# Moving 22 weight loads of one stage from SyncE's DMA queue to GpSimd's

## The chip, the cores and the metric

The kernel runs on one core of one Trainium2 chip. The metric is the device time of one execution in microseconds, lower is better. TensorE is called PE here, VectorE DVE, ScalarE ACT, GpSimd POOL and SyncE SP, as in the profile.

## The reference

A block of three parts, all in float32, on 2304 tokens (4 batches of 576) with a model width of 512.

```python
# 1. random-feature attention, 8 heads of 64, 128 features (q, k already scaled)
phi = lambda x: exp(h - max(h)) / sqrt(128)      # h = x @ omega.T - |x|^2 / 2
num = phi(q) @ (phi(k).T @ v);  den = phi(q) @ sum(phi(k)) + 1e-6
x = num / den                                     # 2304 x 512
# 2. a feed-forward net with 2048 hidden columns
h = x @ w_in;  x = (h * sigmoid(h)) @ w_out
# 3. a gated one with 1536 hidden columns
g = x @ w_gate;  x = (g * sigmoid(g) * (x @ w_val)) @ w_out2
```

The weights come as float64, so each number in HBM is two 32-bit words.

## The kernel before

The matrix products of parts 2 and 3 are done with seven half-size products in place of eight (Strassen's scheme in Winograd's form): an operand is cut into four blocks A11, A12, A21, A22, four sums S1 to S4 of them are made, and seven of these pieces are used. Each piece is kept as two TensorE operands, a rounded "hi" and the remainder "lo", and three matmuls (hi·hi, hi·lo, lo·hi) give a float32-like product.

The program runs five stages one after the other: attention (to about 118 us of the span), **up 1** (`x @ w_in`, to about 290 us), down 1 (with `w_out`), up 2 (`w_gate`, `w_val`) and down 2. Up 1 walks over 24 steps (eight column blocks `i` of `w_in` by three token blocks `s`), in the order blocks 0 to 2, then 3, then 4, then 5 to 7, all three token blocks for each group; a step is seven products `p` (order 1, 5, 6, 2, 7, 3, 4) of six matmuls at L1133. Within a step the partial sums in PSUM are copied from bank to bank by ACT (`copy`, L1150) before TensorE may add the next product to them, so an ACT copy that is late stops TensorE.

Beside its products, up 1 converts weights, in the stream "conv" (`conv_job`). One job takes one block of a weight matrix:

- `load(h)`, L344: two DMAs of 512 KB (h = 0 and 1) bring the two-word numbers into a raw buffer. There are two raw buffers, three once the x operands are made (about 162 us).
- `first(h)`, L368 on ACT, then `shift(h)`, L375 and `low(h)`, L382 on DVE: put the two words together to a float32. `low` gives the raw buffer back.
- `sums(n)`, L401 on POOL, four times: S1, S3, S2, S4 into a buffer `S` of which there is one only, so the next job's S1 waits until this job is done with it.
- For a `w_in` block: `hi` (L433 on DVE, L435 on ACT) and `lo` (L448 on DVE) make the operands that up 1 uses soon after. For a `w_out`, `w_gate` or `w_val` block: `store` (L465, three DMAs on SP) puts the pieces to a DRAM scratch, to be loaded again later.

The jobs in up 1 are in 3, out 3, in 4, out 4, in 5, out 5, in 6, out 6, in 7, out 7, gate 0, val 0. The two loads of the first, in 3, are issued ahead of the stage.

The order of every engine's instructions is fixed when the program is built. A small model keeps a clock for each engine (`clk`), one for the DMA engines, and times `T` at which pieces are ready; `Stream.best` emits, among the heads of a stream's queues (one queue for each engine, in the order that `weave` gives), the one that can start first. For a load the model takes `t` from the engine's clock, adds 0.35 us of issue, starts the transfer no sooner than `t + 1.55` and adds a margin of 1 us (2.5 us for gate and val) to the end before ACT's `first` is planned. On the chip each engine then runs its list strictly in order and waits on semaphores. `weave` puts the two loads of job n+1 ahead of the sums and stores of job n:

```python
for n, j in enumerate(jobs):
    new = deque(jobs[n + 1][:8] ...)        # load 0, load 1, first 0, first 1, shift, low, ...
    for _ in range(min(2, len(new))): ops.append(new.popleft())
    for i, o in enumerate(j[8:]):           # sums 1, 3, [stores], 2, 4, [store] or hi, lo
        ops.append(o)
        if i % 2 and new: ops.append(new.popleft())
    ops += new
```

So SP's queue of the stream holds loads and stores, POOL's holds the sums. SP also issues, in the same list, all other transfers: the results of up 1 (`put`, L1159, `g_d`), the weights of down 1 from the scratch (`down_ops`, L1312, `wd_out`, then L1316 on ACT and L1320 on DVE), and the first inputs of down 1 (`zload`, L1341, only once the stream "conv" is empty; then L1367 on ACT and L1371 on DVE).

Of the kernel before, what the change touches and what calls it, by code (L numbers as in the profile page):

```python
# [11 lines left out]
U32 = mybir.dt.uint32  # L12
# [30 lines left out]
def kernel(  # L43
# [13 lines left out]
    nc = tc.nc  # L57
    ctx.enter_context(tc.manual_schedule())
    P = 128
# [3 lines left out]
    S = 576  # L63
# [16 lines left out]
    FP = (w_in.shape[0], w_gate.shape[0])  # L80
    wsrc = {"in": w_in, "out": w_out, "gate": w_gate, "val": w_val, "out2": w_out2}
    wsrc = {k: w.bitcast(U32) for k, w in wsrc.items()}
# [6 lines left out]
    wd_d = {k: tc.dram_tile([7, P, FP[m] * 256], F32, name=f"wd_{k}") for m, k in enumerate(DNK)}  # L89
    wu_d = {k: tc.dram_tile([P, 7 * 256], F32, name=f"wu_{k}") for k in UPK[1]}  # L90
# [12 lines left out]
    def cut(t, o, n):  # L103
        return t[:, o : o + n]
# [39 lines left out]
    clk = {e: 0.0 for e in ("PE", "ACT", "DVE", "POOL", "SP", "dma", "slot", "landed")}  # L144
# [3 lines left out]
    def cost(kind, n):  # L148
        a, b = fixed[kind]
        return a + b * n  # L150

    class Op:
        __slots__ = ("eng", "cost", "fn", "ins", "outs", "guard", "then", "slots", "live", "lead")

# [20 lines left out]
        def emit(self):  # L175
            t = max(clk[self.eng], self.ready())
            clk["slot"] = 0.0
            if self.eng == "SP":
                took, lag = self.cost
                clk["SP"] = t + 0.35  # L180
                clk["dma"] = max(t + 1.55, clk["dma"]) + took
                clk["end"] = clk["landed"] = clk["dma"] + lag
            else:
                clk["end"] = t + self.cost
            self.fn()
            if self.eng == "SP":
                end = clk["landed"]
            else:
                clk[self.eng] = end = t + self.cost
            for k in self.outs:  # L190
                T[k] = end
            if self.then is not None:
                self.then(end)
# [3 lines left out]
    def dma_cost(nbytes, kind="rows"):  # L197
        a, b = RATE[kind]
        return nbytes * a, b
# [125 lines left out]
    f_raw = Free("raw", [cut(fa, R_AT + i * 1024, 1024) for i in range(2)])  # L325
# [8 lines left out]

    halved = []

    def conv_job(kind, i, dram=None, side=False):
        b = {}
        key = lambda *k: (kind, i, *k)

        def load(h):
            def go():
                b["r", h] = r = f_raw.take()
                nc.sync.dma_start(out=r.bitcast(U32), in_=wsrc[kind][i, h])  # L344

            def then(end):

                if kind != "out2":
                    T[key("r", h)] = end + (1 if kind in ("in", "out") else 2.5)
                else:  # L350
                    T[key("r", h)] = end + 6.0

            return Op("SP", dma_cost(P * 4096, "words"), go, outs=[key("r", h)], slots=(f_raw, 1), then=then)

        def word(h, w):
            return b["r", h].bitcast(U32).rearrange("p (c w) -> p c w", w=2)[:, :, w]
# [32 lines left out]
        def blk(n):  # L389
            if n in ("A21", "A22"):  # L390
                return cut(b["c", 0], 0 if n == "A21" else 256, 256)
            if n in ("A11", "A12"):
                return cut(b["c", 1], 0 if n == "A11" else 256, 256)
            return cut(b["S"], 256 * (int(n[1]) - 1), 256)

        def sums(n, l, r, ins):
            def go():
                if n == 1:
                    b["S"] = f_sum.take()
                f = nc.gpsimd.tensor_add if n == 1 else nc.gpsimd.tensor_sub  # L400
                f(blk(f"S{n}"), blk(l), blk(r))  # L401

            return Op(
                "POOL", cost("POOL", 256), go, ins=[key(*k) for k in ins], outs=[key("S", n)],
                slots=(f_sum, 1) if n == 1 else None,
            )


        parts = ((0, 1), (1, 3), (3, 5), (5, 7))
        after = ([("f", 0)], [("f", 1)], [("S", 1), ("S", 2)], [("S", 3), ("S", 4)])  # L410

        def src(k):
            if k == 0:
                return blk("A22")
            return b["c", 1] if k == 1 else cut(b["S"], 512 * (k - 2), 512)

        def done(t):
            f_c.give(b["c", 0], t)
            f_c.give(b["c", 1], t)
            f_sum.give(b["S"], t)  # L420
# [34 lines left out]
            eng = "POOL" if side else "DVE"  # L455
            return Op(eng, cost(eng, n), go, ins=[key("hi", k)], outs=outs)

        def store(a, z, src, ins):

            b["stores"] = 3  # L460

            def go():
                o = dram(a, z)
                t = src()
                nc.sync.dma_start(out=o, in_=t.rearrange("p (o c) -> p o c", c=256) if len(o.shape) == 3 else t)  # L465
                b["stores"] -= 1
                if not b["stores"]:
                    done(clk["landed"])

            return Op("SP", dma_cost(P * (z - a) * 1024, "parts"), go, ins=[key(*x) for x in ins], outs=[key("d", a)])  # L470

        half = [load(0), load(1), first(0), first(1), shift(0), low(0), shift(1), low(1)]
        if dram is not None:
            return [
                *half,
                sums(1, "A21", "A22", [("f", 0)]),
                sums(3, "A11", "A21", [("f", 0), ("f", 1)]),
                store(0, 1, lambda: blk("A22"), [("f", 0)]),
                store(1, 3, lambda: b["c", 1], [("f", 1)]),
                sums(2, "S1", "A11", [("f", 1)]),  # L480
                sums(4, "A12", "S2", [("f", 1)]),
                store(3, 7, lambda: b["S"], [("S", n) for n in range(1, 5)]),
            ]
        f0, f1 = ("f", 0), ("f", 1)
        return [
# [25 lines left out]
    def weave(*jobs):  # L511

        ops = [*jobs[0][:8]]
        for n, j in enumerate(jobs):
            new = deque(jobs[n + 1][:8] if n + 1 < len(jobs) else ())
            for _ in range(min(2, len(new))):
                ops.append(new.popleft())
            for i, o in enumerate(j[8:]):
                ops.append(o)
                if i % 2 and new:  # L520
                    ops.append(new.popleft())
            ops += new
        return ops

    def down_job(m, i):
        k = DNK[m]
        return conv_job(
            k, i, dram=lambda a, z: wd_d[k][a:z, :, i * 256 : (i + 1) * 256].rearrange("o p c -> p o c")
        )

    def up_job_dram(k):
        return conv_job(k, 0, dram=lambda a, z: wu_d[k][:, a * 256 : z * 256])

    early = {"conv": deque(), "x": deque()}

# [184 lines left out]
    def u_of(u, b):  # L720
        return u // UB, UB * (u % UB) + b
# [185 lines left out]
    def store(u):  # L907
        B, p = u_of(u, 0)
        for b in range(UB):
            T["xd", B, p + b] = 0.0  # L910
            made["xd", B, p + b] = (step_of[0], 3, "out")
        nc.sync.dma_start(
            out=x_d[B][p : p + UB].rearrange("b p s -> p b s"), in_=xts.pop(u).rearrange("p (b s) -> p b s", b=UB)
        )
# [5 lines left out]
    for t in spare_c:  # L920
        f_c.give(t, 0.0)
    f_sum.give(spare_sum, 0.0)
    early["conv"].extend(chain(*(conv_job("in", i, side=True) for i in range(3)), *(down_job(0, i) for i in range(3))))
    early["x"].extend(x_prep(0, 0, xr1, False, "POOL", early=True))
    def two_steps(d):
# [78 lines left out]
    first_up = conv_job("in", 3)  # L1004
    for x in first_up[:2]:
        x.emit()
    for f, some in ((f_c, spare_c), (f_sum, [spare_sum])):
        n = len(f.q)
# [588 lines left out]
        lambda: x_prep(0, 2, xr2, False, "DVE", before=1, then=xr2_end),  # L1597
    ]

    rest = deque(down_job(0, i) for i in range(3, FP[0]))  # L1600
    jobs = []
    for i in range(3, FP[0]):
        jobs += [conv_job("in", i) if i > 3 else first_up, rest.popleft()]
    jobs += rest
    jobs += [up_job_dram("gate"), up_job_dram("val")]
    conv1 = [x for x in weave(*jobs) if not any(x is y for y in first_up[:2])]
    opened = []
    extra_c, extra_raw = cut(fa, XR_AT, 512), cut(fa, XR_AT + 512, 1024)
# [108 lines left out]
    jobs = []  # L1717
    for i in range(1, FP[1]):
        jobs += [conv_job("gate", i), conv_job("val", i), down_job(1, i - 1)]
# [75 lines left out]
```

## Time and profile before

| | |
|---|---|
| three runs | 827.64, 827.8 (median), 830.42 us |
| the profiled execution | 828.38 us, of which the span from first to last instruction is 826.6 us |
| granted TensorE clock | 1.000 of full speed |

The profile shows one execution. "Busy" is the time in which an engine executes; a wait is the idle time of an engine ahead of an instruction, put down to what ended it. Rows marked SPq or ACTq are the engine's sequencer: for a DMA the time that its issue took. Times in a timeline count from the span's start.

### The profile page before, as it was taken

To read this page: it belongs to the slowest core of one execution; us is meant where nothing else is said; L and a number is where in the kernel's file an instruction comes from. 1 tells how busy PE (TensorE), PEld (TensorE's weight loads), DVE (VectorE), ACT (ScalarE), POOL (GpSimd) and SP (SyncE) were. 2 spreads that over 40 slices of the span, in tenths; PEclk is the share of its full clock that TensorE was granted. 3 is DMA by queue.
4 is the path that set the end of the run, shared out by engine and by line. 5 is a ranking of instruction groups with operands and counts; after the bars stand their busy time and mean duration, and the time that the engine had idled before them with its cause. 6 is when DMAs were issued, how large, how long until landed. Compare 5 with 4: busy or idle time off the path is not lost.

```text
span 826.6 us, 18058 instructions
## 1 busy us (share of the span) xinstructions
PE 814.5 (99%) x6889; PEld 794.8 (96%) x6889; DVE 615.1 (74%) x982; ACT 558.5 (68%) x1172; POOL 162.4 (20%) x204
## 2 busy tenths in 40 slices
PE   8999999999999999999999999999999999999998
PEld 7878889999999999999999999999999999999998
DVE  4888877657744598995989987675656559998872
ACT  6989978867767776455577776665656558655552
POOL 0477851033442000000000113130303020000000
PEclk9999999999999999999999999999999999999999
DMA  8679956679889996538366836463636278764502
GB/s 281 197 249 277 315 186 218 201 223 328 288 266 374 395 306 213 170 115 267 116 212 230 271 102 211 126 213 105 212 107 216 101 235 318 250 217 140 164 3 77
DMA packets 112134, 175.58 MB, mean 212 GB/s; under 512 B 9648, under 2 KB 94256, under 8 KB 112048
## 3 DMA queue, kind: packets, MB, share of 16 engines
q1 hardware_dynamic: 111824, 174.20, 63.7%
q8 instruction: 54, 0.88, 0.4%
q10 hardware_dynamic: 224, 0.23, 0.1%
q14 instruction: 32, 0.26, 0.1%
HBM read 109.38 MB, written 65.01 MB: 211 GB/s over the span
## 4 chain that ended last, share of the span: by engine, by line
PE 81%; issue 6%; ACT 4%; DMA 4%; DVE 2%; POOL 1%; SPq 1%; ACTq 0%; DVEq 0%; POOLq 0%
PE ps L1133 36%; PE ps L1556 35%; PE ps L777 3%; ACT kq L793 2%; PE ps L821 2%; PE ps L837 2%; PE ps L868 2%; DMA fa<-in_moe_w_out 1%; POOL fa L401 1%; DMA g_d<-fa 1%; DMA ra<-wd_out 1%; PE ps L893 1%; DMA rawq<-in_q 1%; DVE fa L382 1%; ACT qp L839 1%
## 5 line engine op out<-in xcount | busy, mean ns | idle before, releaser
L401 POOL TENSOR_TENSOR fa<-fa 128x256 f32<-128x256 f32 x124 | 103.4, 848 | 496.2 <-DMA x_d<-fa 202.9
L1133 PE MATMUL ps<-ra 128*128 128x384 f32 x840 | 143.0, 327 | 2.2 <-ACT ps L1150 2.2
L1133 PE MATMUL ps<-rb,ra 128*128 128x384 f32 x840 | 142.4, 327 | 0.8 <-ACT ps L1150 0.8
L1133 PE MATMUL ps<-rc,ra 128*128 128x384 f32 x840 | 141.1, 326 | 0.0
L1133 PEld LDWEIGHTS ps<-ra 128*128 128x128 f32 x840 | 137.1, 189 | 3.5 <-ACT ps L1150 3.5
L1133 PEld LDWEIGHTS ps<-rb,ra 128*128 128x128 f32 x840 | 137.2, 189 | 2.0 <-ACT ps L1150 1.9
L1133 PEld LDWEIGHTS ps<-rc,ra 128*128 128x128 f32 x840 | 137.2, 189 | 0.0
L1150 ACT ACTIVATE ps<-ps 128x384 f32<-128x384 f32 x180 | 85.8, 478 | 67.2 <-PE ps L1133 58.1
L1367 ACT ACTIVATE ra<-fa 128x768 fp32r<-128x768 f32 x81 | 68.0, 843 | 64.2 <-PE ps L1556 55.1
L1556 PE MATMUL ps<-ra,rb 128*128 128x384 f32 x576 | 96.5, 326 | 0.0
L1556 PEld LDWEIGHTS ps<-ra,rb 128*128 128x128 f32 x576 | 94.1, 189 | 0.0
L1371 DVE TENSOR_TENSOR ra<-fa,ra 128x768 fp32r<-128x768 f32 x80 | 76.2, 954 | 19.6 <-ACT ra L1367 18.9
L793 ACT ACTIVATE kq<-ps,nb 128x128 f32<-128x128 f32 x288 | 79.4, 408 | 6.2 <-DVE nb L791 6.1
L1207 DVE TENSOR_TENSOR fa<-fa,ps 128x384 f32<-128x384 f32 x78 | 43.0, 552 | 35.7 <-ACT ps L1150 26.2
L1556 PE MATMUL ps<-ra 128*128 128x384 f32 x414 | 69.2, 326 | 0.0
L1556 PE MATMUL ps<-ra,rc 128*128 128x384 f32 x402 | 68.8, 326 | 0.0
L1556 PEld LDWEIGHTS ps<-ra 128*128 128x128 f32 x414 | 67.6, 189 | 0.0
L1556 PEld LDWEIGHTS ps<-ra,rc 128*128 128x128 f32 x402 | 65.9, 189 | 0.0
L1391 DVE TENSOR_TENSOR fa<-ra,fa 128x768 f32<-128x768 f32 x63 | 60.1, 954 | 0.9 <-DMA ra<-g_d 0.4
L382 DVE SCALAR_TENSOR_TENSOR fa<-fa 128x512 uint32<-128x512 uint32 x65 | 58.7, 903 | 0.7
L368 ACT ACTIVATE fa<-fa 128x512 f32<-128x512 f32 x65 | 54.3, 838 | 4.4 <-DMA fa<-in_moe_w_out 2.7
L791 DVE TENSOR_REDUCE nb<-ps 128x4 f32<-128x512 f32 x72 | 48.4, 682 | 6.3 <-PE ps L777 3.2
(128 smaller groups left out, 1153.2 us busy)
## 6 DMA issues: line engine op xcount, KB each, us to landing
g_d<-fa SPq DMA_DIRECT2D x110, 192.0 KB, 3.8
fa<-g_d SPq DMA_DIRECT2D x42, 384.0 KB, 4.6
ra<-g_d SPq DMA_DIRECT2D x42, 384.0 KB, 4.0
fa<-in_moe_w_out SPq DMA_DIRECT2D x28, 512.0 KB, 5.2
g_d<-mf SPq DMA_DIRECT2D x58, 192.0 KB, 3.9
fa<-in_moe_w_in SPq DMA_DIRECT2D x16, 512.0 KB, 5.2
wd_out<-fa SPq DMA_DIRECT2D x12, 512.0 KB, 3.3
fa<-in_moe_w_gate SPq DMA_DIRECT2D x12, 512.0 KB, 4.1
```

The source lines that it names most:

```text
L368: nc.scalar.activation(c, word(h, 1).bitcast(F32), AF.Prelu, scale=2.0**-112, alpha=-(2.0**32))
L382: nc.vector.scalar_tensor_tensor(c, word(h, 0), 29, c, op0=ALU.logical_shift_right, op1=ALU.bitwise_or)
L401: f(blk(f"S{n}"), blk(l), blk(r))
L791: nc.vector.reduce_max(nb, x, axis=AX.X, negate=True)
L793: nc.scalar.activation(e[:, g // 2, g % 2, h * M : (h + 1) * M], x[:, g, :], AF.Exp, bias=nb[:, g : g + 1])
L1133: nc.tensor.matmul(woven(ps[b][:, :N]), cut(l, j * P, P), halves(cut(r, j * N, N)), start=start and c == 0, stop=stop and c == 5, skip_gro ...
L1150: nc.scalar.activation(out() if callable(out) else out, src, AF.Copy)
L1207: nc.vector.tensor_add(t, t if in_place else p5[n], ps[bank_][:, :N])
L1367: nc.scalar.activation(ops[s, p, k][0], src(), AF.Copy)
L1371: nc.vector.tensor_sub(l, src(), h.bitcast(F32))
L1391: (nc.gpsimd if eng == "POOL" else nc.vector).tensor_sub(z(PLACE[to]), z(PLACE.get(l, l)), z(PLACE.get(r, r)))
L1556: nc.tensor.matmul(woven(ps[BANKS[p] + e][:, :N]), cut(a, e * P, P), halves(b), start=p in FIRST and i == 0 and c == 0, stop=p in LAST and ...
```

## The change

In up 1 the loads of the conversion's words are issued by POOL on its own DMA queue; all other transfers stay on SP's. These are the 22 loads of out 3, in 4 to val 0; those of in 3 are issued ahead of the stage as before, and the conversions in attention and in up 2 keep SP (`own=""`). In the model a load now takes 1.0 us of POOL's clock, and it stands in POOL's queue of the stream, among the sums, in the order that `weave` gives. The code can also put the stores of S (`"S"`) on POOL, which is not used.

```diff
+    ISSUE = {"SP": 0.35, "POOL": 1.0}
...
-            if self.eng == "SP":
+            if isinstance(self.cost, tuple):
                 took, lag = self.cost
-                clk["SP"] = t + 0.35
+                clk[self.eng] = t + ISSUE[self.eng]
                 clk["dma"] = max(t + 1.55, clk["dma"]) + took
...
-    def conv_job(kind, i, dram=None, side=False):
+    def conv_job(kind, i, dram=None, side=False, own=""):
...
                 b["r", h] = r = f_raw.take()
-                nc.sync.dma_start(out=r.bitcast(U32), in_=wsrc[kind][i, h])
+                (nc.gpsimd if "L" in own else nc.sync).dma_start(out=r.bitcast(U32), in_=wsrc[kind][i, h])
...
-            return Op("SP", dma_cost(P * 4096, "words"), go, outs=[key("r", h)], slots=(f_raw, 1), then=then)
+            return Op("POOL" if "L" in own else "SP", dma_cost(P * 4096, "words"), go, outs=[key("r", h)], slots=(f_raw, 1), then=then)
...
-    rest = deque(down_job(0, i) for i in range(3, FP[0]))
+    OWN = "L"
+    rest = deque(down_job(0, i, OWN) for i in range(3, FP[0]))
     jobs = []
     for i in range(3, FP[0]):
-        jobs += [conv_job("in", i) if i > 3 else first_up, rest.popleft()]
+        jobs += [conv_job("in", i, own=OWN) if i > 3 else first_up, rest.popleft()]
     jobs += rest
-    jobs += [up_job_dram("gate"), up_job_dram("val")]
+    jobs += [up_job_dram("gate", OWN), up_job_dram("val", OWN)]
```

## Rows read from the trace of the kernel before

**Rows 1.** The page: span, and busy time of TensorE.

```profile
span 826.6 us, 18058 instructions
...
PE 814.5 (99%) x6889; PEld 794.8 (96%) x6889; DVE 615.1 (74%) x982; ACT 558.5 (68%) x1172; POOL 162.4 (20%) x204
```

**Rows 2.** Waits of PE in up 1, 118 to 292 us (total us, times, longest).

```profile
PE ps L1133 <- ACT ps L1150: 2.5, 5, 1.2
```

**Rows 3.** Timeline of PE in up 1 (start, us, what, idle before).

```profile
190.35 1.24 PE L1133 MATMUL ps<-ra 128*128 128x384 f32 x6 [0.23 <-ACT ps L1150]
...
195.01 1.24 PE L1133 MATMUL ps<-rb,ra 128*128 128x384 f32 x6 [0.50 <-ACT ps L1150]
...
233.52 1.24 PE L1133 MATMUL ps<-ra 128*128 128x384 f32 x6 [1.19 <-ACT ps L1150]
235.04 10.99 PE L1133 MATMUL ps<-ra 128*128 128x384 f32 x66 [0.28 <-ACT ps L1150]
245.87 1.14 PE L1133 MATMUL ps<-rb,ra 128*128 128x384 f32 x6
```

**Rows 4.** Timeline of ACT, same stretch.

```profile
189.06 0.86 ACT L368 ACTIVATE fa<-fa 128x512 f32<-128x512 f32 x1 [0.65 <-DMA fa<-in_moe_w_in]
...
232.42 0.66 ACT L368 ACTIVATE fa<-fa 128x512 f32<-128x512 f32 x1 [2.49 <-DMA fa<-in_moe_w_out]
```

**Rows 5.** Waits of ACT in up 1, 118 to 292 us.

```profile
ACT fa L368 <- DMA fa<-in_moe_w_out: 2.7, 2, 2.5
...
ACT fa L368 <- DMA fa<-in_moe_w_in: 1.3, 2, 0.6
```

**Rows 6.** Timeline of SP's queue, same stretch.

```profile
181.44 0.45 SPq L344 DMA_DIRECT2D fa<-in_moe_w_in  x1
...
218.95 0.33 SPq L344 DMA_DIRECT2D fa<-in_moe_w_in  x1
...
222.00 3.94 SPq L465 DMA_DIRECT2D wd_out<-fa  x2
225.99 0.50 SPq L344 DMA_DIRECT2D fa<-in_moe_w_out  x1
...
228.40 0.44 SPq L344 DMA_DIRECT2D fa<-in_moe_w_gate  x1
```

**Rows 7.** Timeline of POOL, same stretch.

```profile
182.23 2.93 POOL L401 TENSOR_TENSOR fa<-fa 128x256 f32<-128x256 f32 x4 [3.37 <-DMA wd_out<-fa]
...
220.74 4.80 POOL L401 TENSOR_TENSOR fa<-fa 128x256 f32<-128x256 f32 x4 [5.39 <-DVE ra L448]
229.64 2.91 POOL L401 TENSOR_TENSOR fa<-fa 128x256 f32<-128x256 f32 x4 [4.10 <-DMA wd_out<-fa]
```

**Rows 8.** Line L344, 118 to 292 us (ns min/median/max); all its loads to landing.

```profile
L344 SPq DMA_DIRECT2D fa<-in_moe_w_out x10: 333/480/897, 125.0 to 227.8; - x10
...
DMA to landing us min/median/max: 4.2/5.4/7.5
```

**Rows 9.** Line L401, 118 to 292 us (ns min/median/max).

```profile
L401 POOL TENSOR_TENSOR fa<-fa x48: 726/735/2151, 125.0 to 259.2; 128x256 f32<-128x256 f32 x48
```

**Rows 10.** Busy time by stretch: length, PE, PEld, DVE, ACT, POOL; clock, DMA share, GB/s.

```profile
125.00:262.00 137.00, 134.80 (x824) 133.18 (x823) 89.74 (x162) 103.07 (x218) 42.88 (x48) 1.00 0.80 266
```

**Rows 11.** Timeline: last operands of in 7, and the start of down 1.

```profile
235.35 1.03 DVE L448 TENSOR_TENSOR ra<-fa,ra 128x256 fp32r<-128x256 f32 x2 [0.29 <-ACT ra L435]
...
268.26 0.96 DVE L1371 TENSOR_TENSOR mz<-fa,mz 128x768 fp32r<-128x768 f32 x1 [2.14 <-ACT mz L1367]
...
289.81 2.11 PE L1556 MATMUL ps<-mz,ra 128*128 128x384 f32 x12
```

**Rows 12.** Groups of DVE, 118 to 292 us (busy us, mean ns, idle before).

```profile
L382 DVE SCALAR_TENSOR_TENSOR fa<-fa 128x512 uint32<-128x512 uint32 x24 | 22.1, 921 | 0.4
...
L375 DVE TENSOR_SCALAR fa<-fa 128x512 uint32<-128x512 uint32 x24 | 11.9, 497 | 12.2 <-ACT fa L368 11.6 <-DMA g_d<-fa 0.4
...
L433 DVE CAST ra<-fa 128x512 fp32r<-128x512 f32 x10 | 4.2, 424 | 0.1
```

More of the change, by code (lines that the diff above doesn't have):

```diff
@@ L185, in emit @@
             self.fn()
-            if self.eng == "SP":
+            if isinstance(self.cost, tuple):
                 end = clk["landed"]
@@ L456, in lo, with store @@
             return Op(eng, cost(eng, n), go, ins=[key("hi", k)], outs=outs)
-        def store(a, z, src, ins):
+        def store(a, z, src, ins, eng="SP"):
             b["stores"] = 3
@@ L464, in go @@
                 t = src()
-                nc.sync.dma_start(out=o, in_=t.rearrange("p (o c) -> p o c", c=256) if len(o.shape) == 3 else t)
+                by = nc.gpsimd if eng == "POOL" else nc.sync
+                by.dma_start(out=o, in_=t.rearrange("p (o c) -> p o c", c=256) if len(o.shape) == 3 else t)
                 b["stores"] -= 1
@@ L468, in go @@
                     done(clk["landed"])
-            return Op("SP", dma_cost(P * (z - a) * 1024, "parts"), go, ins=[key(*x) for x in ins], outs=[key("d", a)])
+            return Op(eng, dma_cost(P * (z - a) * 1024, "parts"), go, ins=[key(*x) for x in ins], outs=[key("d", a)])
         half = [load(0), load(1), first(0), first(1), shift(0), low(0), shift(1), low(1)]
@@ L481, in conv_job @@
                 sums(4, "A12", "S2", [("f", 1)]),
-                store(3, 7, lambda: b["S"], [("S", n) for n in range(1, 5)]),
+                store(3, 7, lambda: b["S"], [("S", n) for n in range(1, 5)], "POOL" if "S" in own else "SP"),
             ]
@@ L523, in weave, with down_job, up_job_dram @@
         return ops
-    def down_job(m, i):
+    def down_job(m, i, own=""):
         k = DNK[m]
         return conv_job(
-            k, i, dram=lambda a, z: wd_d[k][a:z, :, i * 256 : (i + 1) * 256].rearrange("o p c -> p o c")
+            k, i, dram=lambda a, z: wd_d[k][a:z, :, i * 256 : (i + 1) * 256].rearrange("o p c -> p o c"), own=own
         )
-    def up_job_dram(k):
-        return conv_job(k, 0, dram=lambda a, z: wu_d[k][:, a * 256 : z * 256])
+    def up_job_dram(k, own=""):
+        return conv_job(k, 0, dram=lambda a, z: wu_d[k][:, a * 256 : z * 256], own=own)
     early = {"conv": deque(), "x": deque()}
```

## The prediction, made before the changed kernel was run

> **What bounds the kernel now.** The page comes first: TensorE is busy for 814.5 us of a span of 826.6 us [rows 1]. The change touches up 1 alone, and whatever it does to the queues, it can give back only idle time of TensorE there. So the second view is what TensorE waits for in up 1: 2.5 us in five waits, every one ended by an ACT copy from bank to bank [rows 2]. That is the ceiling of any gain, 0.3% of the time. The third view, TensorE's timeline, places four of them [rows 3]: 0.23, 0.50, 1.19 and 0.28 us, 2.2 us together (the fifth, the rest of 0.3 us, comes after the loads of the stage). The fourth is ACT's timeline ahead of them. At 232.4 us ACT had stood 2.49 us on `first` (L368), because a `w_out` load had not landed; ACT works in order, the copy that TensorE needs came behind it [rows 4], and the gap of 1.19 us follows. The same pattern, smaller, is at 189.1 us: ACT waits 0.65 us on a `w_in` load, TensorE 0.23. In all ACT waits four times on a load, 4.0 us [rows 5], so 18 of 22 land in time. The loads do touch the end, then, but only through ACT's order. A wait of 2.49 us cost 1.19, one of 0.65 cost 0.23 (with work of ACT in between): a copy bears a delay of 0.42 to 1.30 us before TensorE stands. I use the middle, 0.86.
>
> The fifth view says why that load was late. SP's queue stood 3.94 us on two stores of S, until POOL's four sums were done at 220.74 + 4.80 = 225.54, and the load of out 7 came behind them, at 225.99 [rows 6, 7]. It landed at about 232.4, 6.4 us later, where loads of this stretch take 4.2 to 7.5 us, 5.4 in the median [rows 8].
>
> **The change part by part.** It *removes* 22 issues from SP, at 0.33 us (the least) to 0.48 us (a median) each [rows 8], so 7 to 11 us of SP's time. Queued behind them on SP are stores of `g_d` and reloads of the scratch. None of these ends a wait of TensorE in up 1, which are all ACT's copies [rows 2]; as long as that covers them, they are worth nothing.
>
> It *adds* 22 issues to POOL. The trace has no DMA issued by POOL, so the nearest rows bound the price: below, SP's own issue, 0.33 us [rows 8]; above, the longest instruction of POOL in this stage, 2.15 us, where the median is 0.735 [rows 9]. I take 1.0 us: it is the figure in the changed planner, and it lies between a quick and a disturbed POOL instruction. 22 us more are no load for POOL, busy 42.88 of 137 us [rows 10].
>
> It *moves* each load out of SP's list into POOL's, among the sums. There are three kinds; the first loads, of out 3 and in 4, stand ahead of the stretch with the gaps and are left out.
>
> First, the first halves (h = 0) of out 4 to out 7 and val, five loads. They stood behind the store of S, which waits for S4. Now they stand directly behind S4: for out 7 from 225.54 in place of 225.99, 0.45 us sooner, and 0.45 in the other four cases too. The issue takes 1.0 in place of 0.33. So they land later by x = 1.0 - 0.33 - 0.45 = 0.22 us; with the bounds of the issue x runs from -0.45 to 2.15 - 0.33 - 0.45 = 1.37. Where TensorE already waits, x goes through whole. I count three such places, the gaps at 190, 195 and 233 us: 3 × 0.22 = **0.7 us**. Elsewhere 0.22 is under the 0.86 that a copy bears.
>
> Second, the first halves of in 5, in 6, in 7 and gate, four loads. They went out ahead of the sums of the job before and now stand behind them: in 5 went out at 181.44, the sums of in 4 ran from 182.23 to 185.16; gate went out at 228.40, the sums of in 7 ended at 232.55 [rows 6, 7]. That is about 4 us later. What covers it: the second half of the same job goes out later still (in 7's at 218.95, when `low` gives a raw buffer back), and the job's own sums wait for the one buffer S, until 229.64 for in 7. With the issue of 1.0 and the median landing of 5.4 us (counted from SP's issue of 0.33, so 6.1 in all), in 5 lands at 191.3, while ACT's `first` on it ran at 189.06 [rows 4]. In the old order ACT would stand 2.2 us; but the planner knows of the sums and plans `first` later. I take **0**. If that cover is gone, these four pay as in the first rival.
>
> Third, the second halves. Their trigger, `low` of the job ahead, stays, but POOL's next S1 now stands behind the issue. There is room: in 7's second half went out at 218.95, S1 of out 6 began at 220.74, 1.79 us later [rows 6, 7]; in four other cases it is 1.3 to 1.4 us. An issue of 1.0 us fits: **0**. At 2.15 us the chain of sums and stores would be 0.4 to 0.8 us later in each of four rounds, 2.7 us by in 7. In 7's operand for its first product is done by 235.35 + 1.03 = 236.38. That product starts one step, 42 matmuls, ahead of 245.87; 66 took 245.87 - 235.04 = 10.83, so at 245.87 - 6.89 = 238.98 [rows 3, 11]. Its slack of 2.6 us leaves 0.1 us. Down 1 is further off: its first operand is ready at 269.22, used at 289.81 [rows 11].
>
> **The sum.** 0.7 + 0 + 0. The profiled execution took 828.38 us, the span of 826.6 and 1.8 around it; the sum on it gives 829.1. The median of the runs lies 0.6 below that execution, so against the median it is 827.8 + 0.7 = **828.5 us**.
>
> **A rule against this change.** POOL is slower beside DVE: the four sums from 220.74 took 4.80 us, with DVE's conversion running, the four from 229.64 took 2.91 with DVE nearly idle [rows 7]. DVE also has 34 quick instructions in this stage, L375 and L433, at 0.50 and 0.42 us for 512 columns, where L382 takes 0.92 [rows 12]. The Trainium skill (SBUF — State Buffer, "SBUF: two separate sides") says that GpSimd's cores write the descriptors of a DMA issued from there, and that a DVE copy in a two-port mode locks them out until it ends. No row here shows that yet. By that rule alone a load would wait up to one such instruction, 0.43 us, and the time would be 827.8 + 3 × (0.22 + 0.43) = 829.8.
>
> **The rivals.**
>
> *Late loads, ACT stands (slower).* The place is `first` in ACT's list, the price a landing later by x than planned. It meets the nine first halves of the two kinds above: three pay x whole, six pay x - 0.86. At the bound, x = 1.37, that is 3 × 1.37 + 6 × 0.51 = 7.2 us: 835.0. It counts from 3x + 6(x - 0.86) = 4.1 us, which is 0.5%, about what runs of this kernel can tell from no change: x = 1.03, an issue of 1.8 us. For it: no row shows an issue on POOL, and the planner's margin is 1 us. Against: 18 of 22 land in time, and 1.8 us is far from POOL's median of 0.735.
>
> *POOL is slowed beside DVE (a little slower).* The issue stretches as the sums did, by 4.80 / 2.91 = 1.65: x = 1.65 - 0.78 = 0.87, which costs 3 × 0.87 = 2.6 us and 6 × 0.01: 830.5. For it: the two rows of sums. Against: most sums take their least, 0.735 against 0.726 [rows 9].
>
> *Loads overtake stores (a little faster).* On a queue of its own a load no longer stands behind the stores' bytes in SP's. If the one of 6.4 us takes the 4.2 of the quickest [rows 8], it lands 2.2 us sooner, and if the others gain likewise, all four gaps close: 825.6. For it: the spread of the landings. Against: the same engines move the same bytes, and stores that share them end later. The Trainium skill (DMA: Bandwidth & Descriptors, "Issuing engines are not separate DMA queues") holds that only issue time is saved; by it this gain is nothing, and the time 828.5. No row before can show it: these transfers have one queue.
>
> *The move does nothing that counts.* With x near 0 the gaps stay: 827.8, within the forecast.
>
> **How the numbers follow.** Forecast, x between 0 and 0.4: 0.52. Late loads beyond 0.5%: 0.21. POOL slowed: 0.11. Overtaking: 0.14. Something unpriced, to the good side: 0.02. Faster by over 0.5% needs 4.1 us, more than the 2.5 us of idle in up 1: 0.02. Slower by over 0.5% is the first rival: 0.21. The rest, 0.77, is within 0.5%. The range begins at 826.1 (three gaps, 0.23, 1.19 and 0.28, gone) and ends at 833.5, halfway from 831.9, where late loads begin to count, to their upper price.
>
> **What would show it.** POOL's queue should have 22 DMA issues at L344 of about 1.0 us; 0.33, or over 1.8, moves the sum. Out loads should go out as S4 ends, in and gate first halves some 4 us later than before. ACT's waits at L368 on loads should stay under some 6 us, TensorE's in up 1 under 4. S1 of the out jobs should follow the end of L448, not that of an issue. The landing tells overtaking (near 4.2 us) from slowing (over 6). Down 1 should still start near 290 us. The prediction is wrong if TensorE's waits in up 1 pass 6.6 us, or if time is lost elsewhere, as around the span.

## The result and the profile after

The changed kernel takes 832.97 us (median of six runs, 831.71 to 834.13), the kernel before 827.72 (six runs, 826.53 to 830.42): ratio 1.0067, 95% interval 1.0053 to 1.0081, 0.67% slower. That lies inside the range of the prediction, at its slow end, and outside its likeliest case.

The profiled execution took 831.75 us, 3.4 us more than the one of before (828.38), with 3.4 us more of span. Up 1, from its first product (L1110 before, L1113 after) to the first of down 1, took 289.81 − 118.15 = 171.66 us before and 292.54 − 117.88 = 174.66 us after: 3.0 of the 3.4 us. In the code after, the lines stand two or three further on: load L346, `first` L370, `sums` L403, `hi` L437, `lo` L450, the store of S L468, product L1136, copy L1153.

The page after: span, TensorE, and the second DMA queue.

```profile
span 830.0 us, 18081 instructions
...
PE 815.8 (98%) x6889; PEld 794.9 (96%) x6889; DVE 622.4 (75%) x982; ACT 558.1 (67%) x1172; POOL 172.4 (21%) x226
...
q0 software_dynamic: 3168, 11.54, 4.7%
```

A second queue, q0, now carries the 22 loads. The waits of TensorE and of ACT in up 1, 118 to 292 us (total us, times, longest):

```profile
PE ps L1136 <- ACT ps L1153: 5.0, 6, 1.8
...
ACT fa L370 <- DMA fa<-in_moe_w_in: 5.4, 7, 2.0
ACT fa L370 <- DMA fa<-in_moe_w_out: 4.5, 5, 1.4
...
ACT ra L437 <- POOL fa L403: 3.7, 3, 2.1
...
ACT mz L1370 <- DMA fa<-g_d: 2.7, 1, 2.7
```

The first line answers to [rows 2]: TensorE still waits for nothing but ACT's copies, but 5.0 us instead of 2.5. The others answer to [rows 5]. ACT stood 4.0 us on four loads; it now stands 10.7 us on thirteen (5.4 and 4.5, and 0.8 on val), and 3.7 us on POOL's sums ahead of `hi`, on which it had not stood before. TensorE's timeline places the six gaps:

```profile
184.93 4.23 PE L1136 MATMUL ps<-ra 128*128 128x384 f32 x24 [1.25 <-ACT ps L1153]
202.25 1.24 PE L1136 MATMUL ps<-rc,ra 128*128 128x384 f32 x6 [0.42 <-ACT ps L1153]
213.02 1.24 PE L1136 MATMUL ps<-ra 128*128 128x384 f32 x6 [0.74 <-ACT ps L1153]
221.65 4.17 PE L1136 MATMUL ps<-rc,ra 128*128 128x384 f32 x24 [0.24 <-ACT ps L1153]
239.46 8.07 PE L1136 MATMUL ps<-ra 128*128 128x384 f32 x48 [0.55 <-ACT ps L1153]
272.74 19.78 PE L1136 MATMUL ps<-rc,ra 128*128 128x384 f32 x120 [1.81 <-ACT ps L1153]
```

ACT's timeline shows what stood ahead of the copies of all six: three loads, sums twice, an input of down 1.

```profile
183.83 0.67 ACT L370 ACTIVATE fa<-fa 128x512 f32<-128x512 f32 x1 [1.36 <-DMA fa<-in_moe_w_out]
...
200.29 0.85 ACT L370 ACTIVATE fa<-fa 128x512 f32<-128x512 f32 x1 [1.20 <-DMA fa<-in_moe_w_out]
...
211.85 0.73 ACT L370 ACTIVATE fa<-fa 128x512 f32<-128x512 f32 x1 [1.98 <-DMA fa<-in_moe_w_in]
...
220.59 0.63 ACT L437 ACTIVATE ra<-fa 128x512 fp32r<-128x512 f32 x1 [1.17 <-POOL fa L403]
...
236.86 0.63 ACT L437 ACTIVATE ra<-fa 128x512 fp32r<-128x512 f32 x1 [2.09 <-POOL fa L403]
...
271.46 0.84 ACT L1370 ACTIVATE mz<-fa 128x768 fp32r<-128x768 f32 x1 [2.69 <-DMA fa<-g_d]
```

So 1.25 + 0.42 + 0.74 = 2.41 of TensorE's 5.0 us stand behind loads, 0.24 + 0.55 = 0.79 behind sums, and 1.81 behind the input of down 1.

Why are the sums late? POOL's timeline, one round: the last three sums of out 5, the two loads of out 6, then the sums of in 6.

```profile
207.89 2.29 POOL L403 TENSOR_TENSOR fa<-fa 128x256 f32<-128x256 f32 x3 [0.81 <-DVE fa L384]
210.13 0.57 POOL L346 DMA_DIRECT2D fa<-in_moe_w_out  x1
211.36 0.53 POOL L346 DMA_DIRECT2D fa<-in_moe_w_out  x1 [0.66 <-issue]
217.07 3.48 POOL L403 TENSOR_TENSOR fa<-fa 128x256 f32<-128x256 f32 x4 [5.18 <-DMA wd_out<-fa]
```

The next sums need the one buffer S, and so wait for the store out of it. Before, the same sums of in 6 began like this:

```profile
212.43 2.92 POOL L401 TENSOR_TENSOR fa<-fa 128x256 f32<-128x256 f32 x4 [3.40 <-DMA wd_out<-fa]
```

That was 3.40 us after out 5's S4; now it is 6.9 (210.18 to 217.07), of which POOL spends 1.8 on the two issues. Over the five rounds the stretch from S4 to the next S1 was 3.4 to 4.1 us before and is 5.3 to 6.9 after. The chain of work that ended last runs through it: the last store, 210.21 to 217.0, then the sums, then ACT's `hi` at 220.59, behind which TensorE has its gap of 0.24.

```profile
210.21 6.79 DMA wd_out<-fa
217.07 2.34 POOL fa L403 x3
219.50 1.07 POOL fa L403
220.59 0.63 ACT ra L437
```

The median landing of this 512 KB store of S by kernel shows that it is a pattern (transfers of up 1: count, KB each, median us from issue to landing). Before:

```profile
wd_out<-fa SPq DMA_DIRECT2D x5, 512.0 KB, 3.2
```

After:

```profile
fa<-in_moe_w_out POOLq DMA_DIRECT2D x10, 512.0 KB, 6.1
...
wd_out<-fa SPq DMA_DIRECT2D x5, 512.0 KB, 5.7
```

Last, the line of the loads after, which answers to [rows 8]:

```profile
L346 POOL DMA_DIRECT2D fa<-in_moe_w_out x10: 527/567/751, 125.3 to 228.6; - x10
...
DMA to landing us min/median/max: 4.2/5.8/8.3
```

An issue on POOL takes 0.57 us in the median, 0.53 to 0.75 in all. Two in a row took 1.09 us together (out 4's, at 178.26).

### The profile page after: what moved, and what is told of

It reads as the page before. It is cut to its first block, busy times and chain, and to the rows that moved or that the text cites. A ratio compares the mean times of both kernels' runs of the same rounds, so it can differ in the third digit from the quotient of the medians.

```text
span 830.0 us, 18081 instructions
## 1 busy us (share of the span) xinstructions
PE 815.8 (98%) x6889; PEld 794.9 (96%) x6889; DVE 622.4 (75%) x982; ACT 558.1 (67%) x1172; POOL 172.4 (21%) x226
## 4 chain that ended last, share of the span: by engine, by line
PE 83%; DMA 6%; DVE 4%; ACT 3%; issue 2%; POOL 2%; SPq 0%; ACTq 0%; POOLq 0%; DVEq 0%
PE ps L1136 37%; PE ps L1559 35%; PE ps L780 4%; PE ps L824 2%; PE ps L840 2%; PE ps L871 2%; POOL fa L403 2%; DMA wd_out<-fa 2%; DMA fa<-in_moe_w_out 1%; DVE fa L384 1%; PE ps L896 1%; ACT kq L796 1%; DMA fa<-g_d 1%; DMA fa<-in_moe_w_in 1%; DMA wu_gate<-fa 1%
## 5 line engine op out<-in xcount | busy, mean ns | idle before, releaser
L403 POOL TENSOR_TENSOR fa<-fa 128x256 f32<-128x256 f32 x124 | 101.0, 828 | 427.1 <-ACT mf L1177 211.1
L1136 PE MATMUL ps<-ra 128*128 128x384 f32 x840 | 143.1, 327 | 3.3 <-ACT ps L1153 3.0
L1136 PE MATMUL ps<-rc,ra 128*128 128x384 f32 x840 | 141.6, 326 | 2.5 <-ACT ps L1153 2.5
L1136 PEld LDWEIGHTS ps<-ra 128*128 128x128 f32 x840 | 137.0, 189 | 5.2 <-ACT ps L1153 5.1
L1136 PE MATMUL ps<-rb,ra 128*128 128x384 f32 x840 | 141.7, 326 | 0.1
L1136 PEld LDWEIGHTS ps<-rc,ra 128*128 128x128 f32 x840 | 137.1, 189 | 3.4 <-ACT ps L1153 3.4
L1136 PEld LDWEIGHTS ps<-rb,ra 128*128 128x128 f32 x840 | 137.2, 189 | 0.4 <-ACT ps L1153 0.4
L1153 ACT ACTIVATE ps<-ps 128x384 f32<-128x384 f32 x180 | 85.8, 478 | 68.1 <-PE ps L1136 56.1
L1370 ACT ACTIVATE ra<-fa 128x768 fp32r<-128x768 f32 x81 | 68.1, 843 | 64.5 <-PE ps L1559 49.2
L370 ACT ACTIVATE fa<-fa 128x512 f32<-128x512 f32 x65 | 54.3, 838 | 11.5 <-DMA fa<-in_moe_w_in 5.4
L377 DVE TENSOR_SCALAR fa<-fa 128x512 uint32<-128x512 uint32 x65 | 35.2, 542 | 31.1 <-ACT fa L370 31.1
L1210 DVE TENSOR_TENSOR fa<-fa,ps 128x384 f32<-128x384 f32 x72 | 39.6, 550 | 19.5 <-ACT ps L1153 13.3
```

Source lines behind the costliest of these rows:

```text
L370: nc.scalar.activation(c, word(h, 1).bitcast(F32), AF.Prelu, scale=2.0**-112, alpha=-(2.0**32))
L377: nc.vector.tensor_scalar(c, c, 3, None, op0=ALU.logical_shift_left)
L1136: nc.tensor.matmul(woven(ps[b][:, :N]), cut(l, j * P, P), halves(cut(r, j * N, N)), start=start and c == 0, stop=stop and c == 5, skip_gro ...
L1153: nc.scalar.activation(out() if callable(out) else out, src, AF.Copy)
L1210: nc.vector.tensor_add(t, t if in_place else p5[n], ps[bank_][:, :N])
L1370: nc.scalar.activation(ops[s, p, k][0], src(), AF.Copy)
```

## The experiments

Each ratio is to runs of the kernel before made beside that kernel; their medians lie between 827.37 and 828.57 us. The diffs show the lines that matter, not those that pass `own` along.

**The plan or the queue?** The change does two things: the model makes another plan (a load costs 1.0 us of POOL), and the chip uses another queue. The first kernel is the one after with the loads issued by SP:

```diff
-                (nc.gpsimd if "L" in own else nc.sync).dma_start(out=r.bitcast(U32), in_=wsrc[kind][i, h])
+                nc.sync.dma_start(out=r.bitcast(U32), in_=wsrc[kind][i, h])
```

> The changed plan (the order of PE, ACT and DVE is that of the changed kernel) with all loads issued by SP again, each at its place in the plan. Before is 827.7 us, the change 833.0. Store theory (the loads on a queue of their own move their bytes beside the store of S, which then lands about 2 us later, so each round of the conversion starts later and the first input of down 1 comes late): on one queue the next job's S1 follows S4 by 3.4 to 4.2 us again instead of 4.1 to 5.2, and the time falls to 828 to 830. Plan theory (the new order of ACT's list is what costs): stays at 832 to 834. Late-load theory (issue and descriptors on POOL make the loads land late): falls to 828 to 829 too, but with the loads landing sooner and the store not.

Measured: 828.32 us, ratio to before 0.9998 (0.9985 to 1.0011); TensorE waits 2.7 us in up 1. The store of S and ACT's waits on loads:

```profile
wd_out<-fa SPq DMA_DIRECT2D x5, 512.0 KB, 5.5
...
ACT fa L370 <- DMA fa<-in_moe_w_in: 3.9, 5, 1.2
...
ACT fa L370 <- DMA fa<-in_moe_w_out: 1.1, 2, 0.9
```

The store lands nearly as late as after, and from S4 to the next S1 pass 3.1 to 6.9 us; the store theory had said 3.4 to 4.2. What fell are ACT's waits on loads, from 10.7 to 5.0 us. With these lists the time came back without the store, as the late-load theory had said.

The second is the kernel before, its orders on TensorE, DVE and ACT unchanged, with the 22 loads issued by POOL:

```diff
-                nc.sync.dma_start(out=r.bitcast(U32), in_=wsrc[kind][i, h])
+                (nc.gpsimd if own else nc.sync).dma_start(out=r.bitcast(U32), in_=wsrc[kind][i, h])
```

> The plan of the kernel before (PE, ACT and DVE in exactly its order), and only the issue of the 22 loads moved to POOL, at their places in that plan. Store theory: the gap from S4 to the next S1 grows to 4.1 to 5.2 us as in the changed kernel, time 831 to 834. Plan theory: 827.5 to 828.5, as before. Late-load theory: ACT's waits on loads grow from 4 us to 10 or more, time 831 to 834, with the stores landing as before (3.2 us).

Measured: 832.8 us, ratio 1.0054 (1.0034 to 1.0074); up 1 takes 174.70 us, 3.0 more than before. So the plan by itself costs nothing that can be told, and the queue by itself nearly all. POOL's sums of in 4 and in 5, and what ACT stood on, with the old plan (the last three lines are its waits in up 1: total us, times, longest):

```profile
184.28 3.17 POOL L401 TENSOR_TENSOR fa<-fa 128x256 f32<-128x256 f32 x4 [3.11 <-DMA wd_out<-fa]
...
200.39 3.16 POOL L401 TENSOR_TENSOR fa<-fa 128x256 f32<-128x256 f32 x4 [2.01 <-DMA wd_out<-fa]
...
187.48 0.63 ACT L435 ACTIVATE ra<-fa 128x512 fp32r<-128x512 f32 x1 [1.49 <-POOL fa L401]
...
219.87 0.63 ACT L435 ACTIVATE ra<-fa 128x512 fp32r<-128x512 f32 x1 [1.52 <-POOL fa L401]
...
228.20 0.66 ACT L368 ACTIVATE fa<-fa 128x512 f32<-128x512 f32 x1 [2.49 <-DMA fa<-in_moe_w_in]
...
ACT ra L435 <- POOL fa L401: 4.0, 3, 1.5
ACT fa L368 <- DMA fa<-in_moe_w_in: 3.6, 2, 2.5
...
ACT fa L368 <- DMA fa<-in_moe_w_out: 1.0, 2, 0.7
```

The store lands after 5.3 us. The sums of in 4 begin at 184.28 against 182.23 before [rows 7], those of in 5 at 200.39 against 196.80. ACT, whose list was made for the old times, stands on the sums ahead of `hi` for 4.0 us, and TensorE has gaps behind that at 188.54 (1.32) and 220.93 (0.79). At 196.48 (0.84) ACT had stood 1.46 us on DVE (L1207), as it had for 1.18 us ahead of the gap of 0.50 before [rows 3]. A fourth, 1.19 at 229.29, is a load: in 7's second half went out at 222.75 on POOL instead of 218.95 on SP [rows 6], and landed as ACT's 2.49 us of waiting ended. On loads ACT stands 4.6 us in all, 4.0 before; the late-load theory had asked for 10 or more. So with the old lists it is the late store, by way of the sums, that shows most, and with the new ones the late loads.

**Is it the store, on SP's queue?** After, with the store of S on POOL too:

```diff
-    OWN = "L"
+    OWN = "LS"
```

> The changed kernel with the big store of S (four pieces, 512 KB) on POOL's queue too, where it stands behind S4 and ahead of the next loads. Store theory: store and loads share one queue again, the store goes first, the next S1 follows S4 by under 4.5 us, and the time falls to 829 to 831. Late-load theory: the loads go out one more issue later (about 1.1 us), ACT waits more, 834 or over. Plan theory: near 833, whatever the gap does.

Measured: 836.73 us, ratio 1.0109 (1.0091 to 1.0127); TensorE waits 9.2 us in up 1. ACT's waits on loads of in and out:

```profile
ACT fa L370 <- DMA fa<-in_moe_w_in: 7.5, 6, 3.6
ACT fa L370 <- DMA fa<-in_moe_w_out: 5.3, 3, 2.5
```

The store lands after 4.6 us and POOL stands 4.0 to 5.2 us from S4 to the next S1, less than the 5.3 to 6.9 after; but one more issue of POOL, of 0.80 us, stands ahead of each pair of loads, and ACT waits 14.6 us on loads in all. The store theory's 829 to 831 failed, and the late-load theory's 834 or over came: the rounds got shorter, the loads later, and the time longer.

**The longest gap.** The gap of 1.81 us after lies behind an input of down 1 (L1370). This kernel enters that conversion later:

```diff
+        if n == len(seq1) - 2 and p == 1:
             streams["split"].extend(next(d1))
```

> The changed kernel with the splitting of down 1's first inputs entered one step of up 1 later, so that ACT meets its first of them (L1370) some 5 us later. In the changed kernel ACT stood 2.69 us on it and PE 1.81 us behind that. Store theory (the late end of the conversion shows in this wait): this gap goes, time 831.0 to 831.5, the other gaps of 3.2 us stay. Rival (the DMA engines are full there, and the wait only moves to the next input or to the start of down 1): 832.5 to 833.5.

Measured: 831.48 us, ratio 1.0044 (1.0027 to 1.006). That gap is gone (0.87 us remain at another place), TensorE waits 4.1 us, and ACT 11.3 us on loads. By the medians the gap was 1.5 of the 5.2 us lost, but the two intervals overlap; it is one more conversion that comes late in ACT's list, and not the whole cause.

**Which loads?** First in the plan of after: only the loads for out, gate and val on POOL, or only those for in.

```diff
-        jobs += [conv_job("in", i, own=OWN) if i > 3 else first_up, rest.popleft()]
+        jobs += [conv_job("in", i) if i > 3 else first_up, rest.popleft()]
```

> The changed kernel with only the loads of w_out, w_gate and w_val (14 of the 22) on POOL; those of w_in are back on SP. So far: the plan alone costs nothing (828.3 against 828.1), the queue alone 0.54%, and in the latter S4 is followed by the next S1 after 5.2 to 6.0 us, against 3.4 to 4.1 before. Sharing theory (an out load that leaves POOL right after S4 moves its bytes beside the store of S, and the store, which the next job waits for, lands 2 us later): the gap stays at 5 us or more and the time at 831 to 834. Issue theory (every issue on POOL delays what stands behind it there, and the landing): 14 of 22 issues, so about two thirds of the loss, 831.

> The counterpart: only the 8 loads of w_in on POOL, those of w_out, w_gate and w_val behind the stores on SP as before. Sharing theory: the gap from S4 to the next S1 is 3.4 to 4.2 us again and the time 828 to 829. Issue theory: 8 of 22 issues, about a third of the loss, 829.5 to 830.5. Late-load theory as in the prediction (first halves of in jobs go out behind the sums, some 4 us later, and ACT stands on them): most of the loss stays, 831 or more.

Out only: 844.83 us, ratio 1.0196 (1.0174 to 1.0218). This run answers another question than the one asked: POOL stands 8.5 us on out's second halves, twice, and TensorE 5.8 us on in 7's operand. I read it as in's first half taking the raw buffer that out's second half needs, now that the loads are in two lists of the plan; no run tests that. In only: 829.74 us, ratio 1.002 (1.0005 to 1.0034), where the issue theory had 829.5 to 830.5; the store is back at 3.3 us, and TensorE waits 3.3 us in two gaps, 1.44 behind in 5's first half and 1.85 behind in 7's second. To leave the plan out, both were repeated with the orders of before, only the issuing engine changed (`own="L"` for the one group or the other, as in the second kernel):

> The kernel before with only the loads for out, gate and val issued by GpSimd on its own queue; the loads for in stay on SyncE's; the orders of TensorE, ScalarE and VectorE are those of before. Sharing theory (bytes of the out loads beside the store of S make the store land late and each round of the conversion start late): the store lands after 5 us or more instead of 3.2, GpSimd stands about 5 us or more between the rounds instead of 3.4, and most of the 0.54% of all 22 loads comes back: 830.5 to 832.5. Rival (the loss is the loads for in, which stand behind GpSimd's sums): 828 to 829, store after about 3.3.

> The kernel before with only the eight loads for in issued by GpSimd on its own queue; out, gate and val stay on SyncE's; the orders of TensorE, ScalarE and VectorE are those of before. Sharing theory: the store of S lands after about 3.3 us, GpSimd stands 3.4 to 4.2 us between the rounds, 828 to 829.5. Rival (loads behind GpSimd's sums are the loss): 830.5 to 832.5, with ScalarE waiting over 5 us for in's words.

Out, gate and val alone: 832.19 us, ratio 1.0045 (1.0027 to 1.0062), as the sharing theory said. In alone: 830.76 us, ratio 1.0027 (1.0015 to 1.004): the time is in the range of the rival, but ACT's waits on in, 3.2 us, are under the 5 that it asked for. The same transfers as above, first with out's loads on POOL:

```profile
fa<-in_moe_w_out POOLq DMA_DIRECT2D x10, 512.0 KB, 6.9
...
wd_out<-fa SPq DMA_DIRECT2D x5, 512.0 KB, 5.3
```

then with in's:

```profile
fa<-in_moe_w_in POOLq DMA_DIRECT2D x8, 512.0 KB, 5.8
wd_out<-fa SPq DMA_DIRECT2D x5, 512.0 KB, 3.2
```

With the old orders the store is late where out's loads have their own queue, and only there: they go out in the same moment as the store. The 0.45% holds more than that, though: out's loads land late themselves (6.9 us, 5.3 before), and ACT waits 5.3 us on them (2.7 before) beside 3.2 us on sums (none before). In's loads leave the store alone; with them alone on POOL ACT waits 3.2 us on words of in (1.3 before), and TensorE 4.5 us in all. The two parts, 0.45% and 0.27%, add up to more than the 0.54% of both, but not clear of their intervals.

**Is it the bytes?** Two kernels of the old plan whose 22 loads bring 512 of the 1024 words of each row (half of the words are left out, the other half of the raw buffer is never filled); one issues them on SP, one on POOL:

```diff
-                nc.sync.dma_start(out=r.bitcast(U32), in_=wsrc[kind][i, h])
+                nc.sync.dma_start(out=r.bitcast(U32)[:, : 512 if own else 1024], in_=wsrc[kind][i, h][:, : 512 if own else 1024])
```

> The kernel before with the 22 loads bringing only the first 512 of the 1024 words of each row (the rest of the raw buffer keeps old data, so the weights are not the reference's): the control for the next run. All theories: a little under the kernel before, 826.0 to 828.0, as the late loads land about 1 us sooner.

> The same half loads, issued by POOL in the plan of the kernel before (the plan of the queue-only run). Sharing theory: half the bytes beside the store, so it lands about 1 us sooner than in the queue-only run, the gap from S4 to S1 is 4.0 to 4.6 us, and the loss against the half loads on SP falls from 0.54% to 0.3% or less. Issue theory (what costs is the issue on POOL, whatever the bytes): the gap stays at 5.2 us or more and the loss at 0.5%.

On SP: 826.11 us, ratio 0.9973 (0.996 to 0.9986). On POOL: 827.26 us, 0.9994 (0.998 to 1.0008). With half the bytes the queue costs 1.2 us where it costs 4.7 (832.8 less 828.13) with all of them, and the store lands after 4.0 us on POOL's kernel, between 3.2 and 5.3. The number of issues on POOL was the same; so the issues by themselves are not most of the price, the bytes are. Two limits: half loads land sooner everywhere, which leaves more room to hide a late issue in, and the run doesn't tell the late store from the loads' own late landing, as both shrink.

**Does lateness of the sums alone cost this?** The kernel before, all loads on SP, with the first sum of in 4 to in 7 and gate made four times, 2.2 us more of POOL in each of five rounds, about what the late store takes:

```diff
-                f(blk(f"S{n}"), blk(l), blk(r))
+                [f(blk(f"S{n}"), blk(l), blk(r)) for _ in range(4 if own and n == 1 else 1)]
```

> The kernel before, all loads on SyncE's queue; only, the first sum of each of in 4 to in 7 and of gate is computed four times over, so that every round of the conversion has 3 x 0.73 = 2.2 us more of GpSimd ahead of its second half, about what the late store costs a round. If lateness of the conversion's chain is what TensorE pays for: 830.5 to 833, with TensorE waiting over 4 us in up 1. If the chain has the slack and the loss is the loads' own landing: about 828.

Measured: 833.85 us, ratio 1.0062 (1.0046 to 1.0077); TensorE waits 5.8 us. Late sums alone, with every load and store issued by the same engine in the same order as before and the store at 3.2 us, can cost what the change cost. That shows that lateness of this size is enough, not that it is the part at work after. Not all of it need be waiting. TensorE's longest gap, and the stretches behind it (length, PE, PEld, DVE, ACT, POOL; granted clock, DMA share, GB/s):

```profile
188.84 1.24 PE L1133 MATMUL ps<-ra 128*128 128x384 f32 x6 [2.43 <-ACT ps L1150]
...
190.00:191.00 1.00, 1.00 (x6) 1.00 (x5) 1.00 (x2) 1.00 (x3) 0.39 (x1) 0.58 0.75 248
191.00:192.00 1.00, 1.00 (x5) 1.00 (x4) 1.00 (x2) 0.35 (x2) 0.71 (x1) 0.50 1.00 388
192.00:193.00 1.00, 1.00 (x5) 1.00 (x4) 1.00 (x3) 0.54 (x2) 0.59 (x1) 0.50 0.50 181
193.00:194.00 1.00, 1.00 (x6) 1.00 (x5) 0.97 (x2) 0.28 (x1) 1.00 (x2) 0.71 0.77 260
```

Behind the gap of 2.43 us the granted clock is at 0.50, the level of 1.2 GHz, for some 3 us; the four stretches lose 0.42 + 0.50 + 0.50 + 0.29 = 1.7 us of full-speed work. In the profiled execution that is a part of the 5.0 us lost. It isn't needed for the time, though: this one had a mean clock of 0.998 and took 833.52 us, and two others of the six, at 1.000, took 833.75 and 834.31.

**A version that beats both?** Before, with the planner's margin for out's loads at 2.5 us, as it has for gate and val, so that ACT's `first` comes later in its list:

```diff
-                    T[key("r", h)] = end + (1 if kind in ("in", "out") else 2.5)
+                    T[key("r", h)] = end + (1 if kind == "in" else 2.5)
```

> The kernel before with the planner's margin for the out loads at 2.5 us instead of 1, all loads on SyncE's queue: the loads are entered later behind the store, or ScalarE's conversions later among the copies. If ScalarE's waits for words cost TensorE its 2.5 us in up 1, some of it is saved: 826 to 828. Otherwise 828 to 828.5.

Measured: 833.26 us, ratio 1.0054 (1.0037 to 1.007). A miss. The waits on loads shrink as hoped (the 2.49 us of [rows 4] are 0.57), but the conversions behind them come later too, and in 7's last operand, ready at 236.38 before [rows 11], comes too late:

```profile
239.61 4.20 PE L1133 MATMUL ps<-ra 128*128 128x384 f32 x16 [2.81 <-DVE ra L448]
```

Of the ten kernels here that bring all the words, none is faster than the kernel before.

## Why the prediction was right and wrong

**The number: inside the range by luck.** The sum said 828.5, and 832.97 is 4.5 us more. The range reached to 833.5 only for the first rival at an issue of over 1.8 us, and no issue took that long. Of the signs that I had named, ACT's waits on loads (10.7 us, over 6) and TensorE's waits (5.0, over 4) spoke against the sum; the limit of 6.6 us was not passed, and no time was lost around the span.

**The bound: right.** TensorE waits in up 1 for ACT's copies alone, and 2.5 of the 3.0 us that the stage grew by are in that one line. The other 0.4 us of the span's 3.4, and the difference between 3.4 us in the profiled executions and 5.2 in the medians, are not placed; the profiled run after is 1.2 us below its median, that of before 0.7 above its own.

**The issue of 1.0 us: too dear.** It took 0.57, and 1.09 for two in a row. Where 0.5 to 0.6 us pass between an issue and the next S1, they end with `lo` (S1 starts 0.1 us after it) and are no part of the issue. The driver that the first rival needed, an issue of 1.8 us, never came.

**First kind, 0.7 us: x was too long, and its cover was not there.** With 0.57 in place of 1.0 the formula gives x = −0.21, and the five first halves landed 5.0 to 6.2 us after S4's end, where before it was 5.3 to 6.8: −0.2 in the mean. So behind S4 they came no later than before; yet ACT stood 1.36 and 1.20 us on the first two. For x was measured against the old list. In the new plan the same list of ACT, with the loads on SP, sends out's first halves off 2 to 3 us sooner (176.0, 190.8, 208.0, 225.0 and 241.25, against 178.26, 193.95, 210.13, 227.36 and 243.86), since SP is not held by POOL's sums; that kernel takes 828.32 us. On POOL they are late by that much, and the gaps of 1.25 at 184.93 and 0.42 at 202.25 stand behind the first two, at places where TensorE had not waited before.

**Second kind, 0 us: the cover was not full.** "The planner knows of the sums and plans `first` later" was taken as full cover. The loads went out 5.3 us later for in 5 (186.76 against 181.44) and 8.4 for gate, where I had said 4. After, ACT stood 0.38, 0.24 and 0.52 us on those of in 5, in 6 and in 7, with no gap of TensorE right behind; with in's loads alone on POOL, one of the two gaps was behind such a load (1.44 us). In's loads alone, of both halves, cost 0.27% with the old plan and 0.2% with the new one.

**Third kind, 0 us: failed twice.** POOL's S1 of the out jobs does follow `lo` and not an issue, as forecast (189.77, where `lo`, L450, ended at 189.68). But the second halves of in and gate went out 0.9 to 2.8 us later than before, with the late rounds, and that had no price: in 6's went out at 204.57, where it was 202.63, landed 7.3 us later, and ACT's 1.98 us and TensorE's gap of 0.74 stand behind it. And the rounds came late by the other half of the chain, the store of S, for which the next sums wait: 3.2 to 5.7 us in the median. I had this as a clause against the third rival, "stores that share them end later", and gave it no price. The slack of 2.6 us at in 7 was also read at the wrong consumer. It is TensorE's slack on the operand; but ACT's `hi` stands in ACT's list ahead of copies, and a late sum stops those (2.09 us at 236.86, then the gap of 0.55) long before the operand itself is missed.

**The rivals.** *Late loads, ACT stands* named the place and the direction, at 0.21, with the wrong driver. *POOL slowed beside DVE*: no; the issues run 0.53 to 0.75 us, and a lock of 0.43 (by [rows 12] 0.42 or 0.50) on top of the quickest would be 0.96. The Trainium skill (SBUF — State Buffer, "SBUF: two separate sides") has a DVE copy in a two-port mode lock out GpSimd's descriptors; no row here shows a cost of it. *Loads overtake stores* was right that they overtake, and wrong about who gains: over all of out's loads the median landing was later (6.1 against 5.3), and so was the store's. The Trainium skill (DMA: Bandwidth & Descriptors, "Issuing engines are not separate DMA queues") says that DMAs of all issuing engines interleave on the same 16 engines, and that more issuers save only issue time. The store's 5.7 us fits the first half; the second half is too kind, for 22 issues left SP's list and 5.2 us were lost. By that rule I had priced overtaking at nothing.

**What stays open.** The plan of after with its loads on SP also has a late store, 5.5 us, since there the loads stand ahead of it, and it loses nothing: its loads come earlier, and ACT stands 2.2 us on sums where it stands 3.7 after. So a late store costs where it makes the sums late against ACT's list, and not by itself. In the kernel after, loads stand ahead of more of TensorE's waiting than sums do (2.41 against 0.79 us), but a late round also makes the next loads late, and the 1.81 us behind an input of down 1 are put to neither. How much of the 0.67% is the store and how much the loads behind the sums is therefore not shown; the runs with out's or in's loads alone are of the old plan, and there out's part holds both. Nor was a queue of an engine other than POOL tried for the loads, which would have told the second queue from the place in POOL's list.

## What to carry to other kernels

The second queue brought no load in sooner here (5.8 us in the median, 5.4 before); it took away an order. With a load behind the store on one queue the store landed in 3.2 us, with the load on another queue in 5.3, with half the load there in 4.0: if the next round of a chain waits for that store, moving the load makes it pay for the load's bytes. Whether that costs time is up to the lists: with those of the new plan and the loads on SP a store landing in 5.5 us cost nothing. So price lateness at each engine that takes its list in order: what a late piece costs is not the slack of its last consumer, but that of whatever stands behind it in the first list that waits for it.

## What the runs showed of the hardware

A 512 KB store on SP's queue landed in 3.2 to 3.3 us in the median with a load queued behind it, in 5.2 to 5.7 us with the same load on POOL's queue beside it, in 4.0 us beside half the load, and in 5.5 us where the load stood ahead of it on SP's queue. An issue of a load on POOL took 0.57 us, and two in a row 1.09. A gap of TensorE of 2.43 us (2.81 in the kernel with the other margin) was followed by a granted clock of 0.50, the level of 1.2 GHz, for some 3 us, 1.7 us of full-speed work; gaps of 1.81 us after, and of 2.17 us in the kernel with the store on POOL, were followed by no fall: there the clock was 1.0 over the whole span.
